# Layer 2 of a two-layer linear-attention kernel: tokens regrouped through memory, weight rows in that order, another split of phi between ScalarE and VectorE

## The chip, the cores and the metric

The kernel runs on one core of a Trainium2 chip. The metric is the device time of one execution in microseconds (us), as the median of several runs. The engines are named as in the profile: PE (TensorE, matrix products) with PEld (its weight loads), DVE (VectorE), ACT (ScalarE), POOL (GpSimd) and SP (SyncE, which here issues nearly all DMA transfers). SBUF is the on-chip memory of 128 partitions, PSUM the memory that PE writes, and "memory" is the chip's HBM.

## The reference

Two equal layers on S = 2048 tokens of D = 640 features, H = 32 heads of 20, F = 1728 hidden units, all float32, one set of weights for both layers:

```python
phi = lambda t: jnp.where(t > 0, t + 1, jnp.exp(t)) + 1e-6
def _A_ref(x, wqkv, wo):
    q, k, v = ...                       # x @ wqkv, split into heads
    pq, pk = phi(q), phi(k)
    kv = jnp.einsum("bhsd,bhse->bhde", pk, v)
    z = jnp.einsum("bhsd->bhd", pk)
    num = jnp.einsum("bhqd,bhde->bhqe", pq, kv)
    den = jnp.einsum("bhqd,bhd->bhq", pq, z)[..., None] + 1e-6
    return merged(num / den) @ wo       # heads side by side again
def _B_ref(x, w1, b1, w2, b2):
    h = jnp.maximum(x @ w1 + b1, 0)
    return (h * h) @ w2 + b2

x = A_x
x = x + _A_ref(_layernorm(x), A_wqkv, A_wo)
x = x + _B_ref(_layernorm(x), B_w1, B_b1, B_w2, B_b2)
x = x + _A_ref(_layernorm(x), A_wqkv, A_wo)
x = x + _B_ref(_layernorm(x), B_w1, B_b1, B_w2, B_b2)
```

`phi(t)` is the same as `min(exp(t), 1) + max(t, 0) + eps`, with eps = 1e-6, which is how both kernels compute it.

## The kernel before, in words

**Arithmetic.** Each float32 operand is split into a high and a low part, and each product is made of three passes (`mm3`, L643): high by low, low by high, high by high. Weights, once split, are kept in memory in that form (`kept`) and loaded again as they are needed, each row with its high and its low half.

**Tokens.** The 2048 tokens are 16 tiles of 128, one token to a partition. A layer has an A stage, which goes over the 16 tiles in turn, the end of A, and the MLP (the B stage) over 4 groups of 4 tiles, in which the attention's output is also made.

**The A stage** (the loop over `t`, L985 on) does the following in iteration `t`. PE makes tile `t`'s products with the weights of k and q (`part`, L643; 1280 columns in parts of 512, 512 and 256, for each of 5 chunks of 128 features) and adds to the sums over tokens (`G`, `GT`). ACT and DVE make phi of them (`Phi`: `exp` L746 on ACT, `rest` L754 and L755 on DVE). DVE applies the layernorm to tile `t+2` (`a_apply`, L608). SP loads tile `t+3` and stores phi of q for use in the B stage (`q_store`, L859, four transfers). For six late tiles of layer 2 (8, 9, 11, 13, 14, 15) q is left for the end of A (`late_q`), so their iterations are shorter.

**The transposition.** PE needs the normalised tile with features on partitions. DVE transposes all its 32x32 blocks in place (`blocks_T`, L618: `y<-xt`), and then each block has to go to another partition group: 16 copies of 32x160 for a tile (`blocks_move`, L620 to L631: `z<-y`), on ACT (L631) for all tiles but one in layer 2, on DVE (L629) for that one. Half of them are done an iteration ahead (`move`). ACT and DVE then split `z` into the high and low part of `xT` (`xT_split`).

```python
for j in js:
    for i in part:
        d, v = zv[j * B32 : (j + 1) * B32, :, i, :], yv[i * B32 : (i + 1) * B32, :, j, :]
```

**What loads what.** All loads on SP go in the order of the program, and SP's transfers take eight semaphores in turn: a transfer is issued when the eighth before it has landed. The B stage, and with it the last group of layer 1, is ordered by a planner (`Clock`): lines of work, each a generator with a rank, take their turn by the planner's own costs and due times, as long as buffers are free. Three of its lines use SP there: `ring_line` streams the MLP's weight units (`u<-kept_w`, `wE`, `wF`, `wG`, `wH`, L572) into buffers as they come free; `next_line` loads weights of layer 2's projection (chunks 0 to 2) and its first three token tiles, and makes their transposition; `kq_line` loads chunks 3 and 4. The projection's weights are `kq<-kept_kq` (`load_kq`, L426 to L429), ten transfers of 640 KB, high and low half of each of five chunks:

```python
nc.sync.dma_start(kq[c][:, j].bitcast(F32), kept["kq", c][:, j])
```

**The end of A** sums z over the tokens and spreads it to all partitions (`zbc`, L1228 and L1230), makes the matrices for the attention output (`M`; `Mr<-md`, L1334, brings parts of it back from memory in transfers of 160 KB into 32 partitions each), and makes the late q. In the B stage `b_ops` (L865 to L889) reads phi of q: once for the denominators (times `zbc`) and once to divide by them. `k_post` (L938 on) reads phi of k and splits it into `kh`.

Of the kernel before, what the change touches and what calls it, by code (L numbers as in the profile page):

```python
# [8 lines left out]
F32 = mybir.dt.float32  # L9
R32 = mybir.dt.float32r  # L10
AF = mybir.ActivationFunctionType
ALU = mybir.AluOpType

P = 128
S, D, F = 2048, 640, 1728
H, DH = 32, 20
NT = S // P
DC = D // P
# [5 lines left out]
B32 = 32  # L24
# [3 lines left out]
PHI_EPS = 1e-6  # L28

MB = 4e-6 * P * D  # L30
# [261 lines left out]
def kernel(  # L292
# [11 lines left out]
    nc = tc.nc  # L304
# [39 lines left out]
    def ftile(name):  # L344
        return tmp.tile([P, D], F32, tag="f", name=name, bufs=F_BUFS)
# [9 lines left out]
    kept = {}  # L355

    def keep(key, shape):
        nm = "_".join(map(str, key))
        kept[key] = dram.tile(shape, F32, name=f"kept_{nm}", tag=f"kept_{nm}")
        return kept[key]  # L360
# [28 lines left out]
    class FirstLoads:  # L389
# [6 lines left out]
        def high(self, n):  # L396
            for _ in range(min(n, len(self.pending))):
                (nm, c), raw = self.pending.pop(0)
                if nm == "k":
                    kq[c] = wtile("kq").rearrange("p (j n) -> p j n", j=2)  # L400
                    keep(("kq", c), [P, 2, 2 * D])
                s = slice(0, D) if nm == "k" else slice(D, 2 * D)
                u = kq[c][:, :, s]
                nc.scalar.activation(u[:, 0], raw, AF.Copy)
                self.halves.append((u, raw))
# [15 lines left out]
    first_loads = FirstLoads()  # L421

    def keep_kq(c, j):
        nc.sync.dma_start(kept["kq", c][:, j], kq[c][:, j].bitcast(F32))

    def load_kq(c, j):  # L426
        if j == 0:
            kq[c] = wtile("kq").rearrange("p (j n) -> p j n", j=2)
        nc.sync.dma_start(kq[c][:, j].bitcast(F32), kept["kq", c][:, j])  # L429

    def wk(nm):
        s = slice(0, D) if nm == "k" else slice(D, 2 * D)
# [185 lines left out]
        nc.vector.transpose(out=y, in_=src)  # L618
        return [y]

    def blocks_move(yz, js, vector=False, part=range(P // B32)):
        if len(yz) == 1:
            yz.append(ftile("z"))
        yv, zv = (a.rearrange("p (c j q) -> p c j q", c=DC, q=B32) for a in yz)
        for j in js:
            for i in part:
                d, v = zv[j * B32 : (j + 1) * B32, :, i, :], yv[i * B32 : (i + 1) * B32, :, j, :]
                if vector:
                    nc.vector.tensor_copy(d, v)  # L629
                else:  # L630
                    nc.scalar.activation(d, v, AF.Copy)  # L631
# [37 lines left out]

    x1d = [dram.tile([P, D], F32, name=f"x1_{t}", tag=f"x1_{t}") for t in range(NT)]  # L670
    x2 = [dram.tile([P, D], F32, name=f"x2_{t}", tag=f"x2_{t}") for t in range(NT)]

    def rows(t, ap):
        return ap[t * P : (t + 1) * P, :]
# [12 lines left out]
    def a_apply(t):  # L687
        if t < NT:
            ln_apply(("a", t), xt[t], xt[t])
# [8 lines left out]
    for layer in range(N_LAYERS):  # L698
# [20 lines left out]
        GT_ = ap.tile([P, D], F32, name="GT", tag="GT", bufs=1)  # L719
        acc = ap.tile([P, D], F32, name="acc", tag="acc", bufs=1)  # L720
        xh, kh, rq = {}, {}, {}

        xbanks = list(XB)

# [15 lines left out]
        class Phi:  # L740
# [3 lines left out]
            def exp(self, a, ps):  # L744
                b = a + ps.shape[1]
                nc.scalar.activation(self.e[:, a:b], ps, AF.Exp)  # L746
                self.todo.append((a, b, ps))

            def rest(self, n=9):
                while self.todo and n:  # L750
                    n -= 1
                    a, b, ps = self.todo.pop(0)
                    e = self.e[:, a:b]
                    nc.vector.tensor_scalar(e, e, 1.0, PHI_EPS, op0=ALU.min, op1=ALU.add)  # L754
                    nc.vector.scalar_tensor_tensor(  # L755
                        out=self.r[:, a:b], in0=ps, scalar=0.0, in1=e, op0=ALU.max, op1=ALU.add
                    )
# [73 lines left out]
                vo["v" if i < 3 else "o", c] = u[:, j] if i < 3 else w[:, j]  # L831

        pq, xr, pT, yzp, yzx, xn = {}, {}, {}, {}, {}, {}
        dens, xTb = {}, {}
        wu = Units()

# [28 lines left out]
        def b_ops(t):  # L865

            pr = ftile("pr")
            nc.vector.tensor_tensor(
                out=pr.rearrange("p (i r) -> p i r", i=JB),
                in0=pq[t].rearrange("p (i r) -> p i r", i=JB),  # L870
                in1=zbc[:, None, :].to_broadcast([P, JB, R_]), op=ALU.mult,
            )
            yield
            den = small.tile([P, H], F32, tag="den", name="den")
            nc.vector.tensor_reduce(
                den, pr.rearrange("p (h d) -> p h d", d=DH), axis=mybir.AxisListType.X, op=ALU.add
            )
            dens[t] = den
            yield
            den = dens.pop(t)  # L880
            nc.vector.tensor_scalar(den, den, PHI_EPS, None, op0=ALU.add)
            nc.vector.reciprocal(den, den)
            v = pq[t].rearrange("p (h d) -> p h d", d=DH)
            nc.vector.tensor_tensor(
                out=v, in0=v, in1=den[:, :, None].to_broadcast([P, H, DH]), op=ALU.mult
            )
            yield
            yzp[t] = z = ftile("z")
            nc.vector.transpose(  # L889
                out=z, in_=pq.pop(t).rearrange("p (i c b) -> p c i b", i=JB, b=B32)  # L890
            )
# [46 lines left out]
        def k_post(t, r, between=()):  # L938

            kh[t] = u = xtile("kh")  # L940
            nc.scalar.activation(u[:, 0], r, AF.Copy)
            if t == 0:
                nc.gpsimd.tensor_copy(acc, r)
            elif t not in ON_VECTOR[layer]:
                eng = nc.vector if t == NT - 1 else nc.gpsimd
                eng.tensor_tensor(out=acc, in0=acc, in1=r, op=ALU.add)
            first = t in LOW_FIRST[layer]
            for f in () if first else between:
                f()
            nc.vector.tensor_tensor(out=u[:, 1], in0=r, in1=u[:, 0].bitcast(F32), op=ALU.subtract)  # L950
            for f in between if first else ():
                f()
            if t in ON_VECTOR[layer]:
                nc.vector.tensor_tensor(out=acc, in0=acc, in1=r, op=ALU.add)
# [2 lines left out]

        def move(t, n=P // B32, vector=False):

            if t in yza:  # L960
                blocks_move(yza[t], range(moved.get(t, 0), n), vector)
                moved[t] = n

# [22 lines left out]
        for t in range(NT):  # L986
# [125 lines left out]
            if second:  # L1112
                f.rest()
                a_stats(3)
            elif not early and t + 2 < NT:
                a_apply(t + 2)
                yza[t + 2] = blocks_T(xt[t + 2])
            f.rest()
# [23 lines left out]
            f.exp(n0, ps[:, : D - n0])  # L1142
            if not is_late:
                fq.exp(0, ps[:, D - n0 :])
            f.rest()
            if not is_late:
                fq.rest()
# [76 lines left out]
        for j in range(JB):  # L1224
            p, k = slice(j * B32, (j + 1) * B32), j % 2
            v = psz[j // 2][p, k * R_ : (k + 1) * R_]
            if k == 0:
                nc.scalar.activation(zbc[p], v, AF.Copy)  # L1228
            else:
                nc.vector.tensor_copy(zbc[p], v)  # L1230
        b_den(0)
        for i in range(DC):
            g_part(NT - 1, i)
# [419 lines left out]
        def moved(f):  # L1653
            return "any", (("ACT", 0.34), ("DVE", 0.18 + MOVE)), lambda e: f(e == "DVE")
# [487 lines left out]
        def next_line():  # L2142


            for c in range(3):
                for j in range(2):
                    yield "until", quiet
                    yield "SP", 2 * MB, lambda: load_kq(c, j)
                yield "until", quiet
                yield "f", 1  # L2150
                yield "SP", MB, lambda: a_load(c, x2)
            yield "got",
            for c in range(3):
                it = ln_steps(("a", c), xt[c])
                yield "DVE", 0.95, lambda: next(it)
                yield "POOL", 1.33, lambda: next(it)
                yield "DVE", 0.55, lambda: a_apply(c)
                yield "f", 2
                yield "DVE", cost("DVE", D), lambda: yz0.append(blocks_T(xt[c]))
                for j in range(JB):  # L2160
                    for i in range(JB):
                        yield moved(lambda v: blocks_move(yz0[c], (j,), v, (i,)))
                yield "end f", 1
                if c < 2:
                    yield "ACT", cost("ACT", D), lambda: xT_split(c, yz0[c][1])
                    yield "DVE", cost("DVE", D), lambda: None
                    yield "end f", 1

        def kq_line():
            yield "need", ("T free", NG - 1)  # L2170
            for c in (3, 4):
                for j in range(2):
                    yield "until", quiet
                    yield "SP", 2 * MB, lambda: load_kq(c, j)

        def ring_line():
            while wu.ring:
# [236 lines left out]
```

## Time and profile before

| | |
|---|---|
| median of 3 runs | 1325.16 us (1324.68 to 1325.44) |
| span of the profiled execution | 1323.2 us |
| granted TensorE clock | 1.000 |
| mean DMA rate over the span | 235 GB/s |

The page lists for the profiled execution no time but its span, from the first instruction to the last; the median of the runs is 1.96 us above it. A row such as `L631 ACT ACTIVATE z<-y 32x160 f32<-32x160 f32 x195 | 65.1, 334 | 2.2` says: line 631 of the kernel, on ACT, 195 instructions that read `y` and write `z`, 65.1 us busy in all, 334 ns each on the average, and 2.2 us in which ACT stood idle just ahead of them. A row of the windows has the stretch in us, its length, then the busy time of PE, PEld, DVE, ACT and POOL with their instructions, the granted clock, the share of the 16 DMA engines that was busy, and what they moved in GB/s.

### The profile page before, as it was taken

How to read it: one execution, taken by the hardware profiler on the slowest of the kernel's cores; microseconds unless marked ns; L12 is line 12 of the kernel's file. 1: busy time of each engine (PE TensorE's matmuls, PEld its weight loads, DVE VectorE, ACT ScalarE, POOL GpSimd, SP SyncE). 2: the span in 40 equal slices, each digit the busy share in tenths (PEclk: the TensorE clock that was granted, in tenths of full speed). 3: DMA queues.
4: the chain of work that ended last, by engine and by line, in shares of the span. 5: the costliest groups of instructions: out<-in, count | busy, mean ns of one | idle time of the engine just before them, and what ended most of it. 6: DMA issues, size and time to landing. Idle time of an engine off the chain costs nothing.

```text
span 1323.2 us, 21315 instructions
## 1 busy us (share of the span) xinstructions
PE 1314.5 (99%) x7616; PEld 1176.8 (89%) x7616; DVE 970.0 (73%) x1910; ACT 779.7 (59%) x1773; POOL 146.5 (11%) x194
## 2 busy tenths in 40 slices
PE   9999999999999999999999999999999999999999
PEld 8888899989889899888888899998998998998887
DVE  8989988899886777542467678799987777776323
ACT  5988865745665646442757687556474546455422
POOL 1343410000000000000112132000000000000000
PEclk9999999999999999999999999999999999999999
DMA  6679876596878778799731214276877877876775
GB/s 209 226 271 343 323 236 176 160 331 215 302 247 312 278 256 277 250 355 355 284 100 41 60 41 120 63 214 196 292 248 258 302 263 249 302 271 237 273 288 175
DMA packets 118656, 310.86 MB, mean 235 GB/s; under 512 B 14934, under 2 KB 40150, under 8 KB 118518
## 3 DMA queue, kind: packets, MB, share of 16 engines
q1 hardware_dynamic: 117038, 306.81, 67.7%
q10 hardware_dynamic: 1512, 2.69, 0.7%
q8 instruction: 60, 0.98, 0.3%
q14 instruction: 46, 0.38, 0.1%
HBM read 248.66 MB, written 62.23 MB: 235 GB/s over the span
## 4 chain that ended last, share of the span: by engine, by line
PE 94%; DVE 2%; DMA 2%; issue 1%; ACT 1%; SPq 0%; POOL 0%; DVEq 0%; ACTq 0%; POOLq 0%
PE PS L643 35%; PE PS L1748 27%; PE PS L1599 18%; PE PS L1609 5%; PE PS L1565 3%; PE PS L664 3%; PE PS L1276 1%; PE PS L1305 1%; PE PS L1012 1%; DMA kept_w<-uprep 0%; DMA pqt<-pq 0%; DMA u<-kept_w 0%; DVE uprep L473 0%; DMA x<-x 0%; PE PS L612 0%
## 5 line engine op out<-in xcount | busy, mean ns | idle before, releaser
L1748 PE MATMUL PS<-u,h 128*128 128x512 f32 x1318 | 341.9, 391 | 1.6 <-DMA u<-kept_w 1.6
L631 ACT ACTIVATE z<-y 32x160 f32<-32x160 f32 x775 | 259.1, 334 | 68.3 <-DVE y L618 58.8
L643 PE MATMUL PS<-kq,xT 128*128 128x320 f32 (+2 forms) x1575 | 282.2, 334 | 0.2
L1748 PEld LDWEIGHTS PS<-u,h 128*128 128x128 f32 x1318 | 239.4, 188 | 45.9 <-ACT s L1621 1.3
L643 PEld LDWEIGHTS PS<-kq,xT 128*128 128x128 f32 x1575 | 250.2, 188 | 25.8 <-issue 1.0
L1599 PE MATMUL PS<-tx,u 128*128 128x256 f32 x1152 | 161.7, 283 | 0.8 <-ACT s L1621 0.8
L1599 PEld LDWEIGHTS PS<-tx,u 128*128 128x128 f32 x1152 | 150.9, 191 | 5.1 <-ACT s L1621 1.0
L1677 ACT ACTIVATE hr<-PS,b1sb 128x512 f32<-128x512 f32 x104 | 71.2, 685 | 131.0 <-PE PS L1609 115.3
L1599 PEld LDWEIGHTS PS<-xTb,u 128*128 128x128 f32 x864 | 121.2, 190 | 10.9 <-ACT PS L1627 1.0
L598 POOL TENSOR_SCALAR rs<-mv 128x1 f32<-128x1 f32 x62 | 32.6, 526 | 866.3 <-DVE mv L595 866.2
L1599 PE MATMUL PS<-xTb,u 128*128 128x256 f32 x864 | 126.5, 282 | 0.8 <-ACT PS L1627 0.5
L643 PE MATMUL PS<-kh,xh 128*128 128x512 f32 x480 | 124.5, 392 | 0.1
L643 PEld LDWEIGHTS PS<-kh,xh 128*128 128x128 f32 x480 | 87.0, 188 | 15.2 <-DVE kh L950 0.5
L746 ACT ACTIVATE e<-PS 128x320 f32<-128x320 f32 (+4 forms) x128 | 53.3, 435 | 77.5 <-PE PS L643 68.8
L1683 DVE TENSOR_TENSOR hr<-hr 128x512 f32<-128x512 f32 x63 | 42.9, 687 | 69.8 <-ACT h L1696 69.6
L1748 PE MATMUL PS<-h,u 128*128 128x512 f32 x328 | 93.2, 392 | 0.0
L1696 ACT ACTIVATE h<-hr 128x512 fp32r<-128x512 f32 x104 | 64.4, 628 | 38.3 <-PE PS L1748 37.0
L1609 PE MATMUL PS<-xTb,u 128*128 128x512 f32 x288 | 79.3, 392 | 0.0
L754 DVE TENSOR_SCALAR e<-e 128x320 f32<-128x320 f32 (+4 forms) x128 | 41.8, 326 | 50.9 <-ACT e L746 50.6
L1686 DVE TENSOR_TENSOR h<-hr,h 128x512 fp32r<-128x512 f32 x104 | 70.4, 685 | 6.6 <-ACT hr L1681 4.3
L1631 DVE TENSOR_TENSOR PS<-PS,s 128x256 f32<-128x256 f32 x48 | 20.8, 433 | 68.9 <-ACT PS L1627 68.9
L1748 PEld LDWEIGHTS PS<-h,u 128*128 128x128 f32 x328 | 60.0, 188 | 11.4 <-ACT h L1696 0.2
(172 smaller groups left out, 1911.9 us busy)
## 6 DMA issues: line engine op xcount, KB each, us to landing
u<-kept_w SPq DMA_DIRECT2D x116, 640.0 KB, 5.9
u<-kept_wE SPq DMA_DIRECT2D x48, 512.0 KB, 4.3
u<-kept_wH SPq DMA_DIRECT2D x48, 512.0 KB, 4.5
u<-kept_wG SPq DMA_DIRECT2D x48, 512.0 KB, 5.3
u<-kept_wF SPq DMA_DIRECT2D x48, 512.0 KB, 5.5
x<-x SPq DMA_DIRECT2D x40, 320.0 KB, 5.0
st<-in_B_w_dram SPq DMA_DIRECT2D x26, 320.0 KB, 4.6
x<-xr SPq DMA_DIRECT2D x24, 320.0 KB, 4.6
```

What stands on the lines that cost most here:

```text
L631: nc.scalar.activation(d, v, AF.Copy)
L643: nc.tensor.matmul(ps, a, b, start=first and i == 0, stop=last and i == 2)
L664: nc.tensor.matmul(ps[:, j * 512 : j * 512 + HD], aT[:, k, c, :], w[c][:, l, j * HD : (j + 1) * HD], start=c == 0 and i == 0, stop=c == DC ...
L746: nc.scalar.activation(self.e[:, a:b], ps, AF.Exp)
L754: nc.vector.tensor_scalar(e, e, 1.0, PHI_EPS, op0=ALU.min, op1=ALU.add)
L1599: nc.tensor.matmul(ps, l[:, d], r[:, d], start=start and d == 0 and n == 0, stop=d == 1 and n == 2, skip_group_check=True,)
L1609: nc.tensor.matmul(ps, l[:, k], r, start=False, stop=n == 2, skip_group_check=True)
L1677: nc.scalar.activation(r, ps, AF.Relu, bias=b1sb[:, c : c + 1])
L1683: nc.vector.tensor_tensor(out=r, in0=r, in1=r, op=ALU.mult)
L1686: nc.vector.tensor_tensor(out=h[:, 1], in0=r, in1=h[:, 0].bitcast(F32), op=ALU.subtract)
L1696: yield "ACT", cost("ACT", GT), lambda: nc.scalar.activation(h[:, 0], r, AF.Square)
L1748: nc.tensor.matmul(ps, l, r, start=(first or new) and k == 0, stop=end and k == len(a) - 1, **loose)
```

## The change

All of it is for layer 2 only, but for the form of `zbc`.

1. **Tokens through memory.** For tiles 3 to 15 the block copies go. The normalised tile is stored to memory (`x_store`, one transfer of 320 KB) and read back as four transfers of 80 KB (`x_grouped`), each into 32 partitions: partition group `j` gets the 160 features from 160j on, of all four groups of 32 tokens. One transposition of 32x32 blocks by DVE (`x_turn`) then gives `z` as it is to be. The transposition of tile `t+1` now stands in iteration `t` ahead of the layernorm of tile `t+2`; before, that of tile `t+2` stood right behind it. The first three tiles keep their block copies, in the new order of features (`by_rows`).
2. **Weight rows in that order.** Chunk `c` of the features is now the rows 160a + 32c + b, for a of 0 to 3 and b of 0 to 31, where it was 128 rows in a row. So the kept weights are one tile in memory, and `load_kq` reads each half of a chunk in four transfers of 160 KB into 32 partitions each: 40 in place of 10. The planner charges SP a tuple of one entry for the four.
3. **Phi.** ACT also makes max(t, 0), from PSUM (`AF.Relu`). DVE then makes min(e, 1) + that in one operation from SBUF, in place of two, one of which read PSUM.
4. **Epsilon** is no longer added in phi but where phi is read: as the bias of ACT's copy and as the scalar of a `scalar_tensor_tensor` in `k_post` and `b_ops`, and S times epsilon in `zbc`.

```diff
     def load_kq(c, j):
         if j == 0:
             kq[c] = wtile("kq").rearrange("p (j n) -> p j n", j=2)
-        nc.sync.dma_start(kq[c][:, j].bitcast(F32), kept["kq", c][:, j])
+        v = kept["kq",][j].rearrange("(a c b) n -> a c b n", a=JB, b=B32)
+        for a in range(JB):
+            nc.sync.dma_start(kq[c][a * B32 : (a + 1) * B32, j].bitcast(F32), v[a, c])
...
+        eps = PHI_EPS if layer > 0 else 0.0
+        def with_eps(out, in0, in1, op):
+            if layer == 0:
+                nc.vector.tensor_tensor(out=out, in0=in0, in1=in1, op=op)
+            else:
+                nc.vector.scalar_tensor_tensor(
+                    out=out, in0=in0, scalar=eps, in1=in1, op0=ALU.add, op1=op
+                )
...
                 nc.scalar.activation(self.e[:, a:b], ps, AF.Exp)
+                if layer > 0:
+                    nc.scalar.activation(self.r[:, a:b], ps, AF.Relu)
...
                     e = self.e[:, a:b]
+                    if layer > 0:
+                        v = self.r[:, a:b]
+                        nc.vector.scalar_tensor_tensor(
+                            out=v, in0=e, scalar=1.0, in1=v, op0=ALU.min, op1=ALU.add
+                        )
+                        continue
                     nc.vector.tensor_scalar(e, e, 1.0, PHI_EPS, op0=ALU.min, op1=ALU.add)
...
+        def x_store(t):
+            nc.sync.dma_start(xnd[t], xt[t])
+        def x_grouped(t):
+            if layer > 0 and 3 <= t < NT:
+                grouped[t] = ftile("y")
+                v = xnd[t].rearrange("(i q) (j r) -> j q i r", i=JB, j=JB)
+                for j in range(JB):
+                    nc.sync.dma_start(
+                        grouped[t][j * B32 : (j + 1) * B32].rearrange("q (i r) -> q i r", i=JB), v[j]
+                    )
+        def x_turn(t):
+            if t in grouped:
+                z = ftile("z")
+                nc.vector.transpose(
+                    out=z, in_=grouped.pop(t).rearrange("p (i c b) -> p c i b", i=JB, b=B32)
+                )
+                yza[t] = [z, z]
...
-            nc.scalar.activation(u[:, 0], r, AF.Copy)
+            nc.scalar.activation(u[:, 0], r, AF.Copy, bias=eps)
...
-            if t in yza:
+            if layer == 0 and t in yza:
                 blocks_move(yza[t], range(moved.get(t, 0), n), vector)
...
-            elif not early and t + 2 < NT:
+            elif layer > 0:
+                x_turn(t + 1)
+                if not early and t + 2 < NT:
+                    a_apply(t + 2)
+                    x_store(t + 2)
+            elif t + 2 < NT:
                 a_apply(t + 2)
                 yza[t + 2] = blocks_T(xt[t + 2])
             f.rest()
...
                 fq.exp(0, ps[:, D - n0 :])
+            x_grouped(t + 2)
             f.rest()
...
-                    yield "SP", 2 * MB, lambda: load_kq(c, j)
+                    yield "SP", (2 * MB,), lambda: load_kq(c, j)
```

How this moves instructions, at three places. On SP, in the last group of layer 1 (`u` are the MLP's weight units, `kq` layer 2's projection weights, `xt` its token tiles); before:

```order
L572 DMA u<-kept_wH_780 128x1024
L429 DMA kq<-kept_kq_215 128x1280
L572 DMA u<-kept_w_13_639 128x1280
L572 DMA u<-kept_wG_782 128x1024
L429 DMA kq<-kept_kq_215 128x1280
L572 DMA u<-kept_wF_637 128x1024
L681 DMA xt<-x_0_98 128x640
L429 DMA kq<-kept_kq_228 128x1280
L572 DMA u<-kept_w_12_1083 128x1280
L429 DMA kq<-kept_kq_228 128x1280
L681 DMA xt<-x_1_99 128x640
L429 DMA kq<-kept_kq_234 128x1280
```

and of the change:

```order
L575 DMA u<-kept_wH_792 128x1024
L432 DMA kq<-kept_kq 32x1280 x4
L575 DMA u<-kept_w_13_651 128x1280
L575 DMA u<-kept_wG_794 128x1024
L432 DMA kq<-kept_kq 32x1280 x4
L575 DMA u<-kept_wF_649 128x1024
L687 DMA xt<-x_0_98 128x640
L432 DMA kq<-kept_kq 32x1280 x4
L575 DMA u<-kept_w_12_1095 128x1280
L432 DMA kq<-kept_kq 32x1280 x4
L687 DMA xt<-x_1_99 128x640
L432 DMA kq<-kept_kq 32x1280 x4
```

Each load of `kq` stands where it stood, as four. On SP, in the A stage of layer 2 (`pq<-r` stores phi of q); before:

```order
L681 DMA xt<-x_4_102 128x640
L859 DMA pq_0_7330<-r 32x4x160 x4
L681 DMA xt<-x_5_103 128x640
L859 DMA pq_1_7331<-r 32x4x160 x4
L681 DMA xt<-x_6_104 128x640
```

and of the change (`xn<-xt` is the store, `y<-xn` the four loads):

```order
L687 DMA xt<-x_4_102 128x640
L904 DMA pq_0_7372<-r 32x4x160 x4
L861 DMA xn_117<-xt 128x640
L868 DMA y<-xn_117 32x4x160 x4
L687 DMA xt<-x_5_103 128x640
L904 DMA pq_1_7373<-r 32x4x160 x4
L861 DMA xn_118<-xt 128x640
L868 DMA y<-xn_118 32x4x160 x4
L687 DMA xt<-x_6_104 128x640
```

Five transfers are added for each tile, between the stores of q and the next tile's load. On DVE, in one iteration of that stage; before:

```order
L950 TENSOR_TENSOR kh<-r,kh 128x640
L754 TENSOR_SCALAR e<-e 128x256
L755 SCALAR_TENSOR_TENSOR r<-PS,e 128x256
L608 TENSOR_SCALAR xt<-xt,mv,rs 128x640
L618 STREAM_TRANSPOSE y<-xt 128x640
L754 TENSOR_SCALAR e<-e 128x512
L755 SCALAR_TENSOR_TENSOR r<-PS,e 128x512
L353 TENSOR_TENSOR xT<-z,xT 128x640
```

and of the change:

```order
L735 SCALAR_TENSOR_TENSOR kh<-r,kh 128x640
L774 SCALAR_TENSOR_TENSOR r<-e,r 128x256
L875 STREAM_TRANSPOSE z<-y 128x640
L611 TENSOR_SCALAR xt<-xt,mv,rs 128x640
L774 SCALAR_TENSOR_TENSOR r<-e,r 128x512
L353 TENSOR_TENSOR xT<-z,xT 128x640
```

The transposition has moved ahead of the layernorm, where it now waits for a transfer, and the two operations of phi are one. PE's instructions stand in the same order before and after, in all of the kernel.

More of the change, by code (lines that the diff above doesn't have):

```diff
@@ L400, in high @@
                     kq[c] = wtile("kq").rearrange("p (j n) -> p j n", j=2)
-                    keep(("kq", c), [P, 2, 2 * D])
+                    if c == 0:
+                        keep(("kq",), [2, D, 2 * D])
                 s = slice(0, D) if nm == "k" else slice(D, 2 * D)
@@ L423, in keep_kq @@
     def keep_kq(c, j):
-        nc.sync.dma_start(kept["kq", c][:, j], kq[c][:, j].bitcast(F32))
+        nc.sync.dma_start(kept["kq",][j, c * P : (c + 1) * P], kq[c][:, j].bitcast(F32))
     def load_kq(c, j):
@@ L619, in blocks_T, with blocks_move @@
         return [y]
-    def blocks_move(yz, js, vector=False, part=range(P // B32)):
+    def blocks_move(yz, js, vector=False, part=range(P // B32), by_rows=False):
         if len(yz) == 1:
@@ L624, in blocks_move @@
         yv, zv = (a.rearrange("p (c j q) -> p c j q", c=DC, q=B32) for a in yz)
+        if by_rows:
+            yv = yz[0].rearrange("p (j c q) -> p c j q", c=DC, q=B32)
         for j in js:
@@ L671 @@
     x2 = [dram.tile([P, D], F32, name=f"x2_{t}", tag=f"x2_{t}") for t in range(NT)]
+    xnd = [dram.tile([P, D], F32, name=f"xn_{t}", tag=f"xn_{t}") for t in range(NT)]
     def rows(t, ap):
@@ L833 @@
         pq, xr, pT, yzp, yzx, xn = {}, {}, {}, {}, {}, {}
+        grouped = {}
+        def x_store(t):
[15 more added lines that the diff above has]
+                yza[t] = [z, z]
         dens, xTb = {}, {}
@@ L867, in b_ops @@
             pr = ftile("pr")
[L868 to L871, printed above, removed]
+            with_eps(
+                pr.rearrange("p (i r) -> p i r", i=JB),
+                pq[t].rearrange("p (i r) -> p i r", i=JB),
+                zbc[:, None, :].to_broadcast([P, JB, R_]), ALU.mult,
             )
@@ L883, in b_ops @@
             v = pq[t].rearrange("p (h d) -> p h d", d=DH)
-            nc.vector.tensor_tensor(
-                out=v, in0=v, in1=den[:, :, None].to_broadcast([P, H, DH]), op=ALU.mult
-            )
+            with_eps(v, v, den[:, :, None].to_broadcast([P, H, DH]), ALU.mult)
             yield
@@ L949, in k_post @@
                 f()
-            nc.vector.tensor_tensor(out=u[:, 1], in0=r, in1=u[:, 0].bitcast(F32), op=ALU.subtract)
+            with_eps(u[:, 1], r, u[:, 0].bitcast(F32), ALU.subtract)
             for f in between if first else ():
@@ L1227 @@
             if k == 0:
-                nc.scalar.activation(zbc[p], v, AF.Copy)
+                nc.scalar.activation(zbc[p], v, AF.Copy, bias=S * eps)
             else:
-                nc.vector.tensor_copy(zbc[p], v)
+                nc.vector.tensor_scalar(zbc[p], v, S * eps, None, op0=ALU.add)
         b_den(0)
@@ L2161, in next_line @@
                     for i in range(JB):
-                        yield moved(lambda v: blocks_move(yz0[c], (j,), v, (i,)))
+                        yield moved(lambda v: blocks_move(yz0[c], (j,), v, (i,), True))
                 yield "end f", 1
@@ L2173, in kq_line @@
                     yield "until", quiet
-                    yield "SP", 2 * MB, lambda: load_kq(c, j)
+                    yield "SP", (2 * MB,), lambda: load_kq(c, j)
         def ring_line():
```

## The prediction

> **What bounds the kernel now.** I read the page's first part, then busy time by stage, then the waits of PE and the chain that ended last.
>
> ```profile
> span 1323.2 us, 21315 instructions
> ...
> PE 1314.5 (99%) x7616; PEld 1176.8 (89%) x7616; DVE 970.0 (73%) x1910; ACT 779.7 (59%) x1773; POOL 146.5 (11%) x194
> ```
>
> PE (TensorE) is busy for all but 8.7 us of the span, so no other engine bounds the kernel on the average. Work taken from ACT or DVE pays only where PE waits for it. The windows are: the last token group of layer 1, which loads layer 2's first weights (560 to 666 us); layer 2's A stage, which the change rewrites (666 to 847); the end of that stage (847 to 915); the start of the MLP (915 to 930). Columns are the length, the busy times of PE, PEld, DVE, ACT and POOL, the granted clock, the DMA share and GB/s.
>
> ```profile
> 560.00:666.00 106.00, 106.00 (x588) 92.15 (x586) 42.91 (x80) 50.37 (x116) 4.19 (x9) 1.00 0.85 317
> 666.00:847.00 181.00, 181.00 (x974) 159.72 (x972) 130.91 (x257) 120.69 (x301) 43.88 (x43) 1.00 0.27 74
> 847.00:915.00 68.00, 68.00 (x461) 65.12 (x461) 60.53 (x123) 42.73 (x93) 4.03 (x8) 1.00 0.55 154
> 915.00:930.00 15.00, 13.45 (x77) 11.29 (x76) 13.95 (x24) 7.75 (x14) 0.00 (x0) 1.00 0.91 327
> ```
>
> In the A stage PE is busy 181.00 of 181.00 us, with ACT and DVE at two thirds and DMA at 0.27. In the group before it PE is full too, but DMA is at 0.85. The chain and PE's waits say the same of the stage and of what follows it:
>
> ```profile
> 666.38 180.63 PE PS L643 x969
> ```
> ```profile
> PE PS L1748 <- DMA u<-kept_w: 1.6, 2, 1.2
> ```
>
> One unbroken PE step is the whole A stage; the largest of PE's waits over the span is 1.6 us, twice, for MLP weights, and it is the 1.55 us missing in 915 to 930. All the change can win after 560 us is about that. What it can lose is in the first window, where the weights come from memory at the rate of use.
>
> **The change part by part.** *Block copies and phi.* These groups of the A stage of layer 2 go or change (line, engine, operation, shapes, count, then busy time, mean ns and the idle time before them):
>
> ```profile
> L631 ACT ACTIVATE z<-y 32x160 f32<-32x160 f32 x195 | 65.1, 334 | 2.2
> L746 ACT ACTIVATE e<-PS 128x512 f32<-128x512 f32 x10 | 6.0, 598 | 12.0 <-PE PS L643 11.9
> L754 DVE TENSOR_SCALAR e<-e 128x512 f32<-128x512 f32 x10 | 4.2, 419 | 12.6 <-ACT e L746 12.6
> L755 DVE SCALAR_TENSOR_TENSOR r<-PS,e 128x512 f32<-128x512 f32 x10 | 6.9, 692 | 0.3
> ```
>
> ACT loses 192 or so copies, some 64 us, and gets one Relu per part of a projection. By the exponential of the same tile (598 ns for 512 columns) an iteration of a tile with all its 1280 columns gets 1280/512 x 598 = 1.5 us and loses 16 x 334 = 5.3 us. DVE loses L754, 1280/512 x 419 = 1.0 us per such iteration; the operation that stays reads SBUF in place of PSUM, and I cost it at L755's 692 ns. The transposition becomes one of the same size at another place. Both engines get lighter, PE waited for neither in 181 us: 0 us. If PE's cover were gone, ACT would still have 3.8 us more room per tile. Epsilon as a bias of a copy, or as the scalar of an operation that takes two tensors anyway, adds no instruction: at L755's 692/512 ns per column 640 columns are 0.87 us, what such an operation takes now. At the end of the stage two Relus (q of the late tiles) add at most 2 x 0.6 us to ACT between copies that feed PE; PE is full there (68.00 of 68.00). I take 0, bounds 0 and 0.4 us.
>
> *Tokens through memory.* Per tile SP gets one store of 320 KB and four loads of 80 KB.
>
> ```profile
> pq<-r SPq DMA_DIRECT2D x34, 80.0 KB, 1.8
> xt<-x SPq DMA_DIRECT2D x10, 320.0 KB, 3.0
> ```
> ```profile
> 689.03 1.75 SPq L859 DMA_DIRECT2D pq<-r  x4
> 689.27 0.61 DVE L608 TENSOR_SCALAR xt<-xt,mv,rs 128x640 f32<-128x640 f32 x1 [0.27 <-POOL rs L599]
> 701.73 0.60 DVE L608 TENSOR_SCALAR xt<-xt,mv,rs 128x640 f32<-128x640 f32 x1
> ...
> 775.78 0.61 DVE L608 TENSOR_SCALAR xt<-xt,mv,rs 128x640 f32<-128x640 f32 x1 [0.77 <-POOL rs L599]
> 783.94 0.61 DVE L608 TENSOR_SCALAR xt<-xt,mv,rs 128x640 f32<-128x640 f32 x1 [0.77 <-POOL rs L599]
> ```
>
> SP issues q at 689.03, layernorm is applied at 689.27, so the store follows at 690.8 and lands at 693.8, if it takes the 3.0 us of a load of its size. Four issues of 0.44 us (1.75/4) and a landing of 1.8 to 3.0 us bring the regrouped tile to 697.3 to 698.5, that is 8.1 to 9.3 us after 689.27. DVE reads it ahead of the next application, at 701.73: 3.2 to 4.4 us early, in a stage with DMA at 0.27. Behind the loads SP holds only the load of a tile three iterations ahead. 0 us here; the shorter iterations of the late tiles are a rival below.
>
> *Weight rows.* Now the cost. Each of ten loads of 640 KB into 128 partitions becomes four of 160 KB into 32 partitions each, at the same place of SP's order. Where they stand in the last group of layer 1, and which weight unit is behind them:
>
> ```profile
> L429 SPq DMA_DIRECT2D kq<-kept_kq x5: 426/433/696, 564.7 to 578.2; - x5
> ```
> ```profile
> 574.36 0.70 SPq L429 DMA_DIRECT2D kq<-kept_kq  x1
> 576.82 0.32 SPq L572 DMA_DIRECT2D u<-kept_w  x1
> 577.20 0.46 SPq L429 DMA_DIRECT2D kq<-kept_kq  x1
> 577.71 0.42 SPq L681 DMA_DIRECT2D xt<-x  x1
> 578.18 0.43 SPq L429 DMA_DIRECT2D kq<-kept_kq  x1
> 582.46 0.32 SPq L572 DMA_DIRECT2D u<-kept_wE  x1
> ```
> ```profile
> L572 SPq DMA_DIRECT2D u<-kept_wG x1: 319/319/319, 585.8 to 585.8; - x1
> ...
> DMA to landing us min/median/max: 7.9/7.9/7.9
> ```
> ```profile
> 593.81 0.95 PE L1599 MATMUL PS<-tx,u 128*128 128x256 f32 x6
> ```
>
> The unit wG is issued at 585.8, lands 7.9 us later at 593.7, and the products that use it start at 593.81: no slack. Five halves of kq are ahead of it. How full DMA is there, and what a load into 32 partitions runs at (same columns as above):
>
> ```profile
> 565.00:580.00 15.00, 15.00 (x76) 12.72 (x75) 5.59 (x9) 2.72 (x6) 0.00 (x0) 1.00 0.92 335
> 580.00:593.00 13.00, 13.00 (x76) 11.46 (x75) 7.55 (x16) 9.60 (x23) 0.00 (x0) 1.00 1.02 411
> 621.00:632.00 11.00, 11.00 (x67) 9.80 (x67) 3.51 (x8) 3.13 (x6) 0.79 (x2) 1.00 0.93 341
> 655.00:661.00 6.00, 6.00 (x28) 4.97 (x27) 5.27 (x10) 3.07 (x8) 2.60 (x5) 1.00 0.89 357
> ...
> 864.00:868.00 4.00, 4.00 (x29) 4.00 (x28) 3.90 (x8) 3.47 (x6) 0.00 (x0) 1.00 0.91 279
> 868.00:873.00 5.00, 5.00 (x37) 5.00 (x35) 4.93 (x9) 3.79 (x7) 0.00 (x0) 1.00 1.06 218
> ```
>
> From 580 to 593 the engines are full at 411 GB/s, with loads over 128 partitions. From 868 to 873 they are as full (1.06) and move 218: there run loads of M, 160 KB into 32 partitions each, the form that the change gives to kq. Just before, mixed with stores, it is 279. A half of kq is 655.4 kB: 1.59 us at 411, 3.01 at 218, 2.35 at 279, that is 1.42 or 0.76 us more each. Between the ends I take 238, a third of the way up, since the M loads are nearest in form but their rows are half as long: 2.75 us, 1.16 more. Five of them are 5.8 us (3.8 to 7.1). Free DMA time ahead of wG takes some of it back: in 565 to 580 it is 1.2 us by the share (0.08 x 15) and 2.8 us by the bytes ((411-335)/411 x 15); I take the middle, 2.0, since short packets lower the rate without leaving room. **PE is late at 593.7 by 5.8 - 2.0 = 3.8 us** (3.8 - 2.8 = 1.0 to 7.1 - 1.2 = 5.9).
>
> [...]
>
> The sixth half is issued in 621 to 632, where the same reckoning gives 1.16 more and 0.8 to 1.9 us free: 0.2 us (0 to 0.6). The last four follow the last weights of layer 1:
>
> ```profile
> 649.86 3.10 SPq L429 DMA_DIRECT2D kq<-kept_kq  x4
> ```
> ```profile
> 661.00:666.00 5.00, 5.00 (x25) 4.11 (x23) 2.06 (x4) 3.89 (x12) 0.00 (x0) 1.00 0.00 0
> ```
> ```profile
> 666.14 5.05 PE L643 MATMUL PS<-kq,xT 128*128 128x512 f32 x21
> ```
>
> They end by 661, where DMA falls idle, and at 1.16 us more each (0.76 to 1.42) by 665.6 (664.0 to 666.7). The products start at 666.14, three for each chunk of kq at 5.05/21 = 0.24 us; the fourth chunk is due nine products in, at 668.3, the fifth at 669.0. 0 us, with over 1.5 us to spare at the worst.
>
> Issue costs: 30 more issues of 0.44 us. In 574 to 582 SP has room (578.18 to 582.46 holds none), and eight transfers may be under way at once, by the semaphores that SP's loads take in turn: eight quarters are 1.3 MB, 5.5 us of data at 238, more than the 1.8 us from a small issue to its landing, so no hole opens. Sum: 3.8 + 0.2 = 4.0 us. The profiled span becomes 1327.2 us; 2.0 us lie between the span and the median of the runs (1325.16 - 1323.2), so the median becomes 1329.2.
>
> **The rivals.** *The quarters overlap, or their delay is absorbed.* If consecutive quarters fill both sets of partitions at once, or the free time is 2.8 us at 279 GB/s, what is left is 0 to 1.2 us: about 1325.8, no change that can be told. For it speaks the 279 row. Against it: five microseconds at 218 in which several such loads were queued. It decides if a half takes under 2.45 us (5 x 0.86 - 2.0 = 2.3, plus 0.2). [...]
>
> *The full halving.* 218 GB/s, only the 1.2 us free by the share, 0.6 at the sixth: 7.1 - 1.2 + 0.6 = 6.5 us, 1331.7. For it the 1.06 share of the 218 row; against it that kq's rows are twice as long.
>
> *The round trip is late.* From 775.78 to 783.94, in the late tiles, an application follows the last after 8.2 us in place of 12.5. The round trip of 8.1 to 9.3 us is then up to 1.1 us late, and DVE waits in front of layernorm with all that stands behind it: the phi of the part, the next transposed tile. PE needs that tile most of an iteration later. Only if this room is used up does PE wait, six tiles by 1.1 us at most. Half of that, 3.3 us, on top of the 4.0 gives 1332.5.
>
> *Faster.* The 1.55 us of 915 to 930 vanish because the lighter DVE frees the buffer of that weight sooner, and the kq loads are hidden: 1325.2 - 1.6 = 1323.6, and with the other small waits perhaps under 1322.5. Against it: PE work, not DVE's backlog, starts that chain, and the order there is the same.
>
> **How the numbers follow.** The forecast of 1329.2 has a chance of 0.43, overlap or absorption 0.34, the full halving 0.14, the late round trip 0.05, faster 0.04. About 0.2% (2.65 us) can be told from no change; so slower is 0.43 + 0.14 + 0.05 = 0.62, within it 0.34, faster 0.04. The range goes from 1325.0, where the absorbed case begins, to 1333.5, which takes in the full halving and a late round trip.
>
> **What would show it.** The profile after: the windows between 565 and 593 should show DMA full at about 240 to 300 GB/s where kq loads run, and PE should wait in 575 to 597 for u, 3.5 to 4 us in all, with the start of layer 2's A stage moved from 666 by the whole difference. The A stage itself should still take 181 us with PE full, ACT some 40 us less busy; a wait of DVE for y would show the round trip. The prediction is wrong if the A stage's length changes by over 1 us, or if the kq loads run at 400 GB/s, or if PE's wait stands elsewhere.

## The result: 0.9% slower, and the profile after

The changed kernel takes 1338.13 us (1336.59 to 1339.01, four runs) against 1324.92 us before (1324.21 to 1325.44): a ratio of 1.0094, 95% interval 1.008 to 1.0109. The forecast was 1329.2, with a range to 1333.5. The sign was right, and the size forecast, 4.0 us, a third of the 13.2 that came.

The profiled execution is 13.4 us longer. First the page, then the chain that ended last, from the last group of layer 1 to the end of layer 2's A stage (columns: start, length in us, what):

```profile
span 1336.6 us, 21291 instructions
...
PE 1317.9 (99%) x7616; PEld 1178.6 (88%) x7616; DVE 952.5 (71%) x1830; ACT 736.0 (55%) x1645; POOL 142.9 (11%) x194
```
```profile
566.67 7.83 DMA kq<-kept_kq
574.57 10.76 DMA u<-kept_wF
585.34 8.60 DMA kq<-kept_kq
594.00 6.49 DMA u<-kept_wE
600.63 2.90 PE PS L1648 x12
...
668.01 10.88 PE PS L1797 x48
679.33 178.45 PE PS L648 x954
```

Where the chain of before consists of PE alone in this stretch, it now runs for 34 us from transfer to transfer. A load of kq has to land, then a unit wF that took 10.76 us, another load of kq, and the unit wE, which SP issued at 594.00 (582.46 before). PE's first products of the A stage come at 679.1, 13.0 us later than the 666.1 of before. The waits in PE's timeline (the bracket has the idle time ahead and its cause):

```profile
585.46 0.95 PE L1648 MATMUL PS<-tx,u 128*128 128x256 f32 x6 [1.30 <-DMA u<-kept_wF]
...
592.61 1.65 PE L1797 MATMUL PS<-u,h 128*128 128x512 f32 x6 [1.13 <-DMA u<-kept_w]
600.63 1.62 PE L1648 MATMUL PS<-xTb,u 128*128 128x256 f32 x6 [6.37 <-DMA u<-kept_wE]
```

The busy time by stretch, with the columns of the windows (the last three: granted clock, DMA share, GB/s). The first row is of before, the others of the changed kernel:

```profile
570.00:595.00 25.00, 25.00 (x138) 21.61 (x138) 11.08 (x21) 12.02 (x28) 0.00 (x0) 1.00 0.94 366
```
```profile
570.00:595.00 25.00, 21.83 (x114) 18.07 (x112) 10.82 (x21) 10.50 (x23) 0.00 (x0) 1.00 1.03 241
...
596.00:599.70 3.70, 0.00 (x0) 0.00 (x0) 0.00 (x0) 0.00 (x0) 0.00 (x0) 0.98 1.01 309
599.70:606.40 6.70, 5.77 (x20) 5.13 (x21) 0.69 (x1) 1.36 (x4) 0.00 (x0) 0.50 0.84 338
606.40:610.00 3.60, 3.60 (x25) 3.25 (x24) 0.43 (x1) 0.37 (x1) 0.00 (x0) 1.00 0.40 119
...
679.00:860.00 181.00, 180.97 (x973) 159.63 (x970) 116.12 (x188) 73.31 (x162) 40.60 (x43) 1.00 0.43 121
```

DMA is full from 570 to 595 (share 1.03) and moves 241 GB/s in place of 366. PE waits 8.8 us for weights. And when they are there, PE works at half its clock until 606.4. The A stage itself has the length it had, with ACT at 73 us instead of 121.

The 13.4 us are these. 8.8 us are PE's waits above. The products from the unit wE to those of the next wG take 6.19 us (600.63 to 606.82), where before they took 3.67 (590.14 to 593.81): the half clock costs some 2.5 us. PE was already 1.0 us late at 565 (the kq load after wH is issued at 565.74, 564.73 before), by waits of about half a microsecond in layer 1. The run with wide loads, below, has the same layer 1 and not these waits, but others of that kind, so I count them as scatter. 1.1 us are left.

### The profile page after: what moved, and what is told of

Read it like the earlier page. It is cut to its first block, busy times and chain, and to the rows that moved or that the text cites. A ratio compares the mean times of both kernels' runs of the same rounds, so it can differ in the third digit from the quotient of the medians.

```text
span 1336.6 us, 21291 instructions
## 1 busy us (share of the span) xinstructions
PE 1317.9 (99%) x7616; PEld 1178.6 (88%) x7616; DVE 952.5 (71%) x1830; ACT 736.0 (55%) x1645; POOL 142.9 (11%) x194
## 4 chain that ended last, share of the span: by engine, by line
PE 93%; DMA 4%; DVE 2%; ACT 1%; issue 0%; POOL 0%; SPq 0%; ACTq 0%; DVEq 0%; POOLq 0%
PE PS L648 35%; PE PS L1797 27%; PE PS L1648 18%; PE PS L1658 5%; PE PS L1614 3%; PE PS L669 3%; DMA kq<-kept_kq 1%; PE PS L1325 1%; PE PS L1354 1%; DMA u<-kept_wF 1%; PE PS L1055 1%; DMA u<-kept_wE 0%; DMA u<-kept_wH 0%; DMA u<-kept_w 0%; ACT z L636 0%
## 5 line engine op out<-in xcount | busy, mean ns | idle before, releaser
L636 ACT ACTIVATE z<-y 32x160 f32<-32x160 f32 x583 | 195.0, 334 | 65.8 <-DVE y L621 58.5
L774 DVE SCALAR_TENSOR_TENSOR r<-e,r 128x320 f32<-128x320 f32 (+4 forms) x52 | 35.2, 676 | 59.2 <-ACT r L764 59.2
```

## Experiments

Theory A: a load into 32 neighbouring partitions runs at half the rate and holds up the wide loads beside it. Theory B: it is the number of loads, four times as many issues behind eight semaphores. Theory C: the cost is in the rest of the change. Each kernel was timed next to runs of the kernel before on the same chip; a ratio is against those.

**The change with wide weight loads.** Everything of the change stays but the form of the weight rows: chunk `c` takes the features 5p + c, a regular pattern for one load of 128 partitions, and the transpositions read their tile with that step.

```diff
-        v = kept["kq",][j].rearrange("(a c b) n -> a c b n", a=JB, b=B32)
-        for a in range(JB):
-            nc.sync.dma_start(kq[c][a * B32 : (a + 1) * B32, j].bitcast(F32), v[a, c])
+        v = kept["kq",][j].rearrange("(p c) n -> c p n", c=DC)
+        nc.sync.dma_start(kq[c][:, j].bitcast(F32), v[c])
...
-                    out=z, in_=grouped.pop(t).rearrange("p (i c b) -> p c i b", i=JB, b=B32)
+                    out=z, in_=grouped.pop(t).rearrange("p (i b c) -> p c i b", i=JB, b=B32)
...
+                    blocks_T(xt[c].rearrange("p (j b c) -> p j c b", j=JB, b=B32))
```

> The change with all its parts, but each half of a kq chunk comes in one load of 640 KB into 128 partitions again: chunk c takes every fifth feature (5p + c for partition p), the transpositions read their tile with that step, and the rows of a chunk are then one regular pattern. Theory A (loads into 32 partitions run at half the rate and hold up the wide loads beside them): the waits for u at 583 to 600 us go, and the slow clock after them; 1324 to 1326 us. Theory B (four times as many issues, each behind one of eight semaphores, keep SP from issuing wE until 594): these go too, same time; this run does not tell A from B. Theory C (phi, epsilon or the way through memory cost the time): it stays over 1334 us.

Measured: 1325.61 us, ratio 0.9999 (0.9987 to 1.0011). The loss is gone, with all the rest of the change in place, so theory C falls: the way through memory, phi and epsilon together cost nothing that can be told, and bring nothing, to within some 1.5 us. As expected, this run does not tell A from B. The stretch is back at its rate:

```profile
570.00:595.00 25.00, 25.00 (x137) 21.73 (x136) 11.55 (x23) 11.87 (x27) 0.00 (x0) 1.00 0.99 383
```

**Narrow loads alone.** The kernel before, with `load_kq` as four loads of 32 neighbouring partitions:

```diff
-        nc.sync.dma_start(kq[c][:, j].bitcast(F32), kept["kq", c][:, j])
+        for a in range(JB):
+            s = slice(a * B32, (a + 1) * B32)
+            nc.sync.dma_start(kq[c][s, j].bitcast(F32), kept["kq", c][s, j])
```

> The kernel before, with nothing changed but each kq load of 128 partitions split into four loads of 32 partitions one behind the other (rows of a chunk as before). Theories A and B: the whole loss is there, 1335 to 1339 us, PE waits of 6 us and more near 590 to 600 us and the half clock after them. Theory C: 1325 us.

Measured: 1335.25 us, ratio 1.0074 (1.0057 to 1.0091), an interval that overlaps that of the change. The edit by itself makes most of the loss, and by the intervals perhaps all of it, with PE waits of 7.9 us, the same chain (a unit wF, a load of kq, the unit wE, then PE) and 249 GB/s in 570 to 595.

**The same four loads, spread out.** As the last, but each takes every fourth partition: `kq[c][a::JB, j]` from `kept["kq", c][a::JB, j]`.

> The kernel before, each kq load split into four loads of 32 partitions, but of every fourth partition (a, a+4, a+8, ...), so that each of them spreads over the whole height of SBUF: same count, sizes and issues as the other split. Theory A: DMA runs at 400 GB/s and more in 570 to 595, little or no wait, 1324.5 to 1327 us. Theory B: 1335 to 1339 us, as with 32 neighbouring partitions.

Measured: 1327.25 us, ratio 1.001 (1.0 to 1.0019).

```profile
570.00:595.00 25.00, 24.28 (x134) 20.61 (x133) 10.38 (x20) 11.88 (x27) 0.00 (x0) 1.00 0.96 346
```

Same count, size and issues, and 346 GB/s in place of 249, with under 1 us of waiting. The rate is below the 400 that was expected, and the profiled execution, at 1325.28 us, is one of the faster of ten. So the place of the partitions makes most of the loss (theory A), and the number of loads at most 0.1 to 0.2% (theory B falls as the main cause).

**Loads of 64 partitions.** Two loads of 320 KB, partitions 0 to 63 and 64 to 127.

> The kernel before, each of the ten kq loads split into two loads of 64 partitions (0 to 63, 64 to 127) of 320 KB. Theory A (a load into one half of SBUF has half the rate, however many of its partitions it takes): as with four times 32, 240 to 260 GB/s in 570 to 595, a wait of 7 to 10 us, 1333 to 1337 us. Theory D (the number of partitions sets the rate, or the small pieces do): a load of 64 runs clearly faster, a wait of 2 to 4 us, 1327 to 1330 us.

Measured: 1340.04 us, ratio 1.009 (1.0059 to 1.0122).

```profile
570.00:595.00 25.00, 20.00 (x106) 16.62 (x106) 9.94 (x18) 10.50 (x23) 0.00 (x0) 1.00 1.04 208
```

Twice the partitions run no faster: 208 GB/s in the profiled execution, which is the slowest of the four (1333.17 to 1343.34 us). The time is above both expectations, but its interval overlaps that of four times 32, so whether 64 is worse than 32 stays open. Theory D falls. So it is not how many partitions a load takes: 64 neighbours do no better than 32 (208 and 249 GB/s in 570 to 595), while 32 spread over all 128 do (346).

**Quarters in another order.** The change as it is, with `for a in (0, 2, 1, 3)`.

> The change as it is, but the four loads of a half go to the partition groups in the order 0, 2, 1, 3 (first 0 to 31, then 64 to 95, then 32 to 63, then 96 to 127). If neighbouring loads to the two halves of SBUF overlap (the rival of overlap, with the right neighbours), the rate in 570 to 595 rises from 240 towards 320 to 400 GB/s and the time falls to 1326 to 1332 us. [...]

Measured: 1335.03 us, ratio 1.0063 (1.0043 to 1.0084). In the profiled execution, the fastest of the four (1331.65 to 1337.12 us), the rate is 304 GB/s, and the longest wait 3.6 us in place of 6.4:

```profile
570.00:595.00 25.00, 21.44 (x115) 18.34 (x114) 10.38 (x20) 10.50 (x23) 0.00 (x0) 0.98 1.03 304
```

So in this execution neighbouring loads to the two halves seem to overlap in part. The rate falls short of the expected 320, the median lies above the expected 1326 to 1332 us, and its interval overlaps that of the change, so whether the order gains time stays open. The rate of the whole mix, wide loads included, was 26% above that of the changed kernel (304 over 241), one execution of each, and still far from the 383 of wide loads.

**Three narrow loads, apart and together.** The kernel before. Only the three halves ahead of the late unit are split, first where they stand, with a weight unit and a token tile of 128 partitions between them; then as twelve loads in a row, those two ahead of them.

```diff
+        parts = 4 if (c, j) in ((1, 0), (1, 1), (2, 0)) else 1
+        for a in range(parts):
+            s = slice(a * P // parts, (a + 1) * P // parts)
+            nc.sync.dma_start(kq[c][s, j].bitcast(F32), kept["kq", c][s, j])
```

> The kernel before, only three of the ten kq loads split into four times 32 partitions: the three ahead of the late weight unit (chunk 1 high and low, chunk 2 high), a token tile and a weight unit of 128 partitions between them as before. By the sum of the prediction, in which only the narrow loads pay: 3 x 1.16 (at most 1.42) less 0.7 to 2 us of free time, so PE waits 1.5 to 3.5 us and it takes 1326.5 to 1329 us. If wide transfers among and behind the narrow ones pay as well (theory A2: they run at about 300 GB/s): a wait of 4 to 6.5 us, 1329 to 1332 us. [...]

> As the run with three narrow kq loads, but these are issued one behind the other, as twelve loads in a row at the place of the third; the weight unit and the two token tiles that stood among them go ahead of them. Same bytes, same number of loads. If only the narrow loads pay: the same wait as with the three apart. Theory A2: fewer wide transfers stand among narrow ones, so the wait falls by 1 to 2.5 us against the three apart.

Measured: apart 1334.63 us, ratio 1.0057 (1.004 to 1.0074), with one wait of 7.3 us; together 1331.47 us, ratio 1.0035 (1.0022 to 1.0048), with one wait of 3.1 us. The same bytes in the same number of loads cost less than half the wait when no wide load stands among them: 4.1 us less, where 1 to 2.5 were expected. The rates, first apart, then together:

```profile
578.00:582.00 4.00, 4.00 (x25) 3.52 (x24) 2.69 (x5) 1.76 (x6) 0.00 (x0) 1.00 1.05 261
582.00:586.00 4.00, 4.00 (x30) 3.74 (x29) 2.84 (x6) 2.54 (x7) 0.00 (x0) 1.00 1.03 216
586.00:590.00 4.00, 4.00 (x20) 3.34 (x19) 1.93 (x5) 3.33 (x7) 0.00 (x0) 1.00 0.96 218
590.00:593.00 3.00, 0.86 (x4) 0.38 (x2) 1.82 (x4) 1.65 (x5) 0.00 (x0) 1.00 0.80 218
```
```profile
580.00:584.00 4.00, 4.00 (x30) 3.74 (x29) 2.79 (x5) 3.26 (x8) 0.00 (x0) 1.00 1.05 283
584.00:588.50 4.50, 4.50 (x24) 3.83 (x24) 2.19 (x6) 2.51 (x6) 0.00 (x0) 1.00 0.69 169
588.50:590.00 1.50, 1.50 (x8) 1.23 (x8) 0.97 (x2) 1.44 (x3) 0.00 (x0) 1.00 0.97 280
```

Apart, DMA stays at 216 to 261 GB/s for 15 us, which is 3.4 MB by these rows (261 x 4 + 216 x 4 + 218 x 7). The three narrow halves are 1.97 MB of it; the other 1.5 MB or so are wide loads, in a mix that as a whole runs near the rate of narrow ones. The records of single packets, the pieces that a DMA engine moves, show that the wide loads are slower too. Packets of 2560 bytes are those of the token tiles alone, loads of 128 partitions: in 570 to 595 their median is 102 ns before, 102 ns in the run with spread loads, and 174 ns in the changed kernel. Theory A2 holds.

Together, there are two more things to see:

```profile
582.00:586.00 4.00, 4.00 (x30) 3.78 (x29) 2.83 (x7) 2.54 (x7) 0.00 (x0) 1.00 1.02 211
586.00:588.00 2.00, 2.00 (x10) 1.63 (x9) 0.22 (x1) 1.42 (x3) 0.00 (x0) 1.00 0.41 133
```

With hardly a wide load among them, narrow loads fill DMA at 211 GB/s. And then a hole follows, a share of 0.41: by the profile SP took 11.1 us to issue the twelve, and stood 2.4 us of that until the weight unit ahead of the twelve had landed, and 1.7 us until the token tile had, before it could issue the next ones. Apart, and in the changed kernel, the share stays near 1 up to 590. The wait of 7.3 us with the three apart is longer than theory A2 had it (4 to 6.5), and the time too (1329 to 1332). It is also nearly the whole wait of the run with all ten split (7.9 us): the two halves of chunk 0, which stand first, cost little.

**The other five.** The kernel before, with the last five halves split (from chunk 2 low on).

> The kernel before, the other end: only the last five kq loads split into four times 32 partitions (chunk 2 low, issued near 621 us, and chunks 3 and 4 near 650 us). By the prediction the sixth costs 0.2 us (0 to 0.6) and the last four nothing, since they land before their products: 1325 to 1326 us, no change. If wide transfers beside them pay too, the weight units after 621 us come later by some 1 us more: up to 1327 us.

Measured: 1326.23 us, ratio 0.9996 (0.9986 to 1.0005), no change. DMA runs beside PE without a wait of PE, here at the last four:

```profile
650.55 12.47 SPq L432 DMA_DIRECT2D kq<-kept_kq  x16
```
```profile
655.00:668.00 13.00, 13.00 (x61) 10.78 (x60) 8.63 (x16) 8.60 (x22) 2.60 (x5) 1.00 0.82 195
```

## Why the prediction was wrong

**What bounds the kernel, and where the change would hurt: right.** PE, full before and after; the loss stands where the first kq loads meet the weight units, and the last products of layer 1 carry it to the end. The unit is another than the prediction's: it set its due time by wG (products at 593.81 before), but PE stood longest for wE, which comes ahead of it (590.14 before), 6.4 of the 8.8 us.

**Block copies, phi, epsilon, tokens through memory, each at nothing: right.** Without the narrow loads the ratio is 0.9999. In the A stage of the changed kernel ACT has 47 us less to do and the stage is as long as before. The round trip is as early as it was reckoned: stores land in 2.2 us and loads in 2.0, and DVE waited for `y` once:

```profile
xn<-xt SPq DMA_DIRECT2D x13, 320.0 KB, 2.2
y<-xn SPq DMA_DIRECT2D x52, 80.0 KB, 2.0
```
```profile
DVE z L875 <- DMA y<-xn: 0.4, 1, 0.4
```

So the rival of a late round trip is out. (Two small slips of the prediction change nothing: by its own rows the way there and back takes 8.0 to 9.2 us, not 8.1 to 9.3, and the row of PE's waits, 1.6, 2, 1.2, means 1.6 us in two waits together, the longer 1.2.) For 512 columns the new operation of phi takes the 692 ns that were stated. In one place phi got dearer than stated, without a consequence, since DVE had room:

```profile
L774 DVE SCALAR_TENSOR_TENSOR r<-e,r 128x384 f32<-128x384 f32 x10 | 15.2, 1524 | 4.8 <-ACT r L764 4.8
```

The operation takes 1.5 us where the one that reads PSUM took 0.56 for the same 384 columns. Why, no run shows.

**The sixth half and the last four: right.** The other five give no change (by the interval, a loss of over 0.7 us is out), and in the changed kernel PE does not wait for the last four either.

**"Five of them are 5.8 us": this step failed.** It was to leave PE 3.8 us late, and PE waited 8.8. The sum as a whole failed in three ways, the first two in this step.

- *Its rate.* 238 GB/s was taken between 218 and 279. Narrow loads ran at 211, with hardly a wide one among them, in the run with the three together, and the mix at 216 to 218 with the three apart. At 218 the term is 7.1 us, 1.3 more. The reason the prediction gave for 2.0 us of free time, that short packets lower the rate, shows little in the trace of before: in 565 to 580 the median packet of 2560 bytes took 102 ns and that of 5120 bytes 196, 4% apart per byte, and the 144 packets of 4 bytes took 9 ns each.
- *What is missing in it.* It charged the narrow loads alone and left the wide ones among them at 411. From 570 to 595 the changed kernel moves 241 x 25 = 6.0 MB. About four narrow halves are in there, 2.6 MB, 12.0 us at 218; the other 3.4 MB then took 13 us, where 411 GB/s makes it 8.3. That is an estimate of 4.7 us, the largest piece of the error. With it the step gives 3.8 + 1.3 + 4.7 = 9.8 us, against 8.8 us of waits. The run with the three apart comes out by the same reckoning: 3 x 1.42 = 4.3 for the narrow loads and 6.7 - 3.6 = 3.1 for 1.47 MB at 218 in place of 411, 7.4 us against a wait of 7.3. That wide loads among narrow ones pay is shown by the two runs with three halves and by the packets of the token tiles; the size in the changed kernel is reckoned.
- *What follows a long wait.* The sum had nothing for PE's clock, which cost some 2.5 us here.

**The second rival, the full halving, was the nearest**, for its rate, but at 1331.7 it left out the same two terms. The first rival, overlap, shows at most in part, and only with the quarters alternated (304 GB/s in one execution); with the quarters in their order the stretch stayed at 241. "No hole opens" held for the changed kernel (share 1.03), not for twelve small loads in a row (0.41).

**The range** to 1333.5 took in the full halving (1331.7) and a late round trip (1332.5); what wide loads among narrow ones lose, and the clock, could not be in it.

## What to carry to other kernels

Look at which partitions a load reaches, not only at its bytes: here loads into 32 or 64 neighbouring partitions brought DMA down to 208 to 249 GB/s from 366, and the wide loads around them became slower with them. Where a layout is to be changed, look for one whose rows are a regular pattern over all partitions: 5p + c did what 160a + 32c + b does, in one load. And add the clock to the price of a long wait of PE: in these runs it was halved after waits of 1.9 and 2.1 us, not after one of 2.3, and after every one of 3.1 us or more.

## What the runs showed of the hardware

After a long wait PE's clock was halved, for 3.4, 6.8 or 10.2 us. The run with the three together (a wait of 3.1 us), the changed kernel (6.4, the rows above) and the run of 64 partitions (8.3):

```profile
595.20:598.50 3.30, 3.30 (x12) 2.82 (x11) 0.69 (x1) 1.36 (x4) 0.00 (x0) 0.50 1.02 409
```
```profile
600.00:610.10 10.10, 5.26 (x19) 4.71 (x19) 0.69 (x1) 1.36 (x4) 0.00 (x0) 0.50 1.00 335
```

The halved stretches are 3.4, 6.8 and 10.2 us long (each row lies just inside its own). They begin between 3.4 us into the wait (run of 64) and more than a microsecond after its end, and last into the work: in the run with the three together the half clock begins at 595.1, more than a microsecond after the wait had ended. Waits of 1.1 to 1.3 us in the changed kernel were not followed by it. Near 2 us both are seen. In the run of 64 a wait of 2.3 us ahead of the long one was not followed by it, and a later one of 1.9 us was:

```profile
940.06 2.79 PE L1751 MATMUL PS<-u,h 128*128 128x512 f32 x8 [1.88 <-DMA u<-kept_w]
```
```profile
942.00:944.00 2.00, 2.00 (x7) 1.62 (x7) 2.00 (x4) 0.00 (x0) 0.00 (x0) 0.50 1.03 421
```

In the run with wide weight loads one of 2.1 us was: the ten products behind it took 4.10 us, where nine of the same line took 2.07 a little later. So the length of the wait alone does not decide. By the clock records of the run of 64 its two stretches begin 341.33 us apart, 100 times a third of the 10.24 us that the first one lasts; in the changed kernel two begin 737.28 us apart (the second behind the last instruction), 216 times half of the 6.83 us of its first. What decides whether a wait is followed by the half clock, no run here shows.

By what the wide loads are held up, no run here shows.
